# A third shifted copy of VectorE's attention tiles, made by GpSimd

## The chip, the cores and the metric

The kernel runs on one core of a Trainium2 chip. The metric is the device time of one execution in microseconds (us), as the median of several executions. The profile is that of one execution, and its times run from the first instruction.

Five engines work side by side, each with its own queue in a fixed order: TensorE (PE; PEld is its weight load), VectorE (DVE), ScalarE (ACT), GpSimd (POOL) and SyncE (SP), which here only starts transfers. They wait for one another on semaphores.

## The reference

Two pre-normalised layers on a sequence of 2048 tokens with 448 features. The first is attention with 16 query heads of 28 features that share one key and one value head. The second chooses 8 tokens by a score and sends them alone through a gated feed-forward net.

```
q = layernorm(x) @ wq            # 16 heads of 28
k, v = layernorm(x) @ wk, @ wv   # one head for all
p = softmax(q @ k.T / sqrt(28))
h = x + (p @ v) @ wo
r = layernorm(h) @ w_r           # 8 best of 2048 tokens
out = h + layernorm(h) + scatter(moe(layernorm(h)[best 8]))
```

Nearly all the time is spent in the scores, their exponential and the product with v: 16 x 2048 x 2048 exponentials.

## The kernel before, in words

**Blocks and tiles.** The attention is cut into 16 blocks (4 heads by 512 queries) and each block into 16 tiles of 128 keys. A tile is 4 heads x 512 queries on 128 partitions. TensorE computes its scores in two halves of 128 x 1024 (two matmuls each, helper line 371), somebody turns them into probabilities, and TensorE multiplies these with v (`Vs`) and adds them up in the bank of the block. A column of `Vs` holds the softmax's denominator.

**Two ways to the exponential.** Most tiles go to ScalarE: `act_unit` (line 880), one ACTIVATE for each half (line 884), written as `P`. Then one group of four products follows (`act_pv`). The others go to VectorE, which has no exponential: `dve_unit` (line 892) evicts each half as a clamped 16-bit integer (line 896) whose bits, read as bf16, are a rough power of two. Its error is smoothed with shifted copies: `shift` (line 900) adds a constant to the integers, and four variants v = 0 to 3, each multiplied with its own multiple of the values, are summed up by TensorE: `dve_pv` (line 907), four groups of four products for each such tile. The copies live in `Y`, with three buffers.

Before, VectorE makes the variants in two instructions (line 902): one of 2048 elements a partition (v = 1 from v = 0) and one of 4096 (v = 2 and 3 from v = 0 and 1).

**Which tiles.** `groups` (line 852) gives the number of VectorE tiles of a block: 4 in each block from 2 on, at the places of `where`; in blocks 0 and 1 together there are 5. That is 61 of 256 tiles; ScalarE has 195.

**Other work in a block.** VectorE also evicts the queries of a later block (`Q`, line 488) and the finished sums (`Ot`, line 658). `post_block` sends the denominators through memory (`Lc`, `Li`, `Rb`), and GpSimd keeps two checks (lines 668 and 670) and forms `On` = `Ot` x `Rb` (line 674). `out_proj` (line 687) makes four rows of the result from four `On` and does a layer norm: VectorE at lines 696 to 713, GpSimd for the power -0.5 (line 702). In the last block `last_pre` (line 793) and what follows it do this, followed by the feed-forward part.

**The order.** No engine's order is written out by hand. Each operation is told to a planner (`_Graph.op`) with an engine, an expected duration in ns, what it reads and writes, and a due time `prio`; 16 units of due time are one block. `plan` (line 79) is a list scheduler: an engine that is free takes, of the operations that are ready, the one with the earliest due time. The resulting order of each engine is fixed, and `finish` puts in the semaphores. At run time only the order counts, not the planned times. A second, exact version of the attention is in the program and is jumped over unless a check fails.

Of the kernel before, what the change touches and what calls it, by code (L numbers as in the profile page):

```python
# [7 lines left out]
ALU = mybir.AluOpType  # L8
# [10 lines left out]
class _Op:  # L19
    __slots__ = ("eng", "fns", "dur", "lat", "deps", "prio", "idx", "dma", "start", "end", "sig", "name", "nsucc",  # L20
                 "pred_left", "succs", "ready", "form")


class _Graph:
# [16 lines left out]
    def op(self, eng, fns, dur, reads=(), writes=(), prio=None, dma=False, acc=False, name="", form=0):  # L41
# [8 lines left out]
        o.form = form  # L50

# [27 lines left out]
    def plan(self):  # L79
# [16 lines left out]
        form = 0  # L96
        while left:
            best = None
            for e, lst in avail.items():
                if not lst:  # L100
                    continue
                t = free[e]
                now = [o for o in lst if o.ready <= t]
# [17 lines left out]
            free[e] = c.end  # L121
            orders[e].append(c)
# [120 lines left out]
def _main(nc, G, sb, ps, psb, flag, scr, xs, ptab, A_x, A_wq, A_wk, A_wv, A_wo, B_w_r, B_w_gate, B_w_up, B_w_down, out,  # L243
# [443 lines left out]
    def out_proj(qb, k):  # L687
# [3 lines left out]
        for g2 in range(0, 4, 2):  # L691
# [15 lines left out]
             reads=[("mv", t), ("h4", hr)], writes=[("h6", hr)])  # L707
        G.op(DV, lambda e: e.tensor_scalar(outf[:, t, :], h, st[:, t, 5:6], s6, ALU.mult, ALU.add), 420,  # L708
             reads=[("h", hr), ("st5", t), ("h6", hr)], writes=[("outf", t)])
        G.op(DV, lambda e: e.scalar_tensor_tensor(junk[:, :], h, s4, w_rb[:, :], ALU.mult, ALU.mult,  # L710
                                                  accum_out=st[:, t, 2:3]), 700,
             reads=[("h", hr), ("h4", hr), "w_rb"], writes=["junk", ("st2", t)])
        G.op(DV, lambda e: e.scalar_tensor_tensor(x_sb[:, t, D + 2:D + 3], s6, sw[:, 0:1], st[:, t, 2:3],
                                                  ALU.mult, ALU.add), 85,
             reads=[("h6", hr), "sw", ("st2", t)], writes=[("r", t)])
# [34 lines left out]
    def second_top():  # L750
        bank = misc_bank(15)
        if exact:
# [7 lines left out]
             reads=["iota96", "qsel", "prow"], writes=["ohq", "posc"])  # L760
# [8 lines left out]
        for src, dst, nm, rd in ((out[0, 0:1536, :], extc[:, 0:D], "extc", [("out", q, k) for q in range(3) for k in (1, 3)]),  # L769
# [5 lines left out]
                                           ALU.add), 420, reads=["hc"] + old, writes=["xnc"])  # L775

    def last_w():
        for g in range(4):
            G.op(DV, lambda e, g=g: e.scalar_tensor_tensor(junk[:, :], wo_pad[:, g, 0:D], 1.0, w_rb[:, :],
                                                           ALU.mult, ALU.mult, accum_out=wor[:, g:g + 1]), 600,  # L780
                 reads=["wo_pad", "w_rb", ("scr0", 3)] + wok, writes=["junk", ("wor", g)])
# [4 lines left out]
        for k in range(4):  # L786
            G.op(DV, lambda e, k=k: e.scalar_tensor_tensor(junk[:, :], x_sb[:, 12 + k, 0:D], 1.0, w_rb[:, :],
                                                           ALU.mult, ALU.mult, accum_out=xw[:, k:k + 1]), 600,
                 reads=[("x", 12 + k), "w_rb", ("scr0", 3)], writes=["junk", ("xw", k)])
# [62 lines left out]
    groups = [4] * NB  # L852
# [47 lines left out]
    def shift(m, v):  # L900
        n = m % NY
        G.op(DV, lambda e: e.tensor_scalar(Y[:, n, v:2 * v, :, :].bitcast(I16), Y[:, n, 0:v, :, :].bitcast(I16),  # L902
                                           v * STEP, None, ALU.add), 70 + 535 * v,
             reads=[("Y", n, 0, 0), ("Y", n, 0, 1)] + ([("Y", n, 1)] if v == 2 else []),
             writes=[("Y", n, 1)] if v == 1 else [("Y", n, 2), ("Y", n, 3)])
# [12 lines left out]
    for m, (b, j, t) in enumerate(dve_tiles):  # L918
        for p in range(2):
            at(t + 1.5 * p, dve_unit, m, b, j, p, t + 1.5 * p)  # L920
        for v in (1, 2):
            at(t + 1.6 + 0.5 * v, shift, m, v)
        for v in range(4):
            pv_list.append((t + 2.2 + 0.5 * v, dve_pv, m, v, b, j))
# [23 lines left out]
    at(16 * 2 + 2.5, q_project, 3, misc_bank(2))  # L948
# [255 lines left out]
```

## Time and profile before

| | |
|---|---|
| median of 3 runs | 404.59 us (404.42 to 405.1) |
| profiled execution | 403.72 us |
| its span, first to last instruction | 401.9 us |
| busy: ScalarE, VectorE, TensorE, GpSimd | 375.6, 354.8, 348.9, 62.2 us |
| granted TensorE clock, mean | 0.977 |

The profile's page gives the busy time of each engine, the costliest groups of instructions (line, engine, operation, output<-input, shapes, count, then busy time in us, mean ns of one, and the engine's idle time before them with what ended it), and the chain of work that ended last. Further views of the same trace are used: the timeline of one engine (start, duration, instruction, and in square brackets the idle time before it and what ended it; equal neighbours are merged, with their count), waits by releaser (total us, times, longest), and a table of stretches (for each, its length, then busy time and number of instructions of PE, PEld, DVE, ACT and POOL, the granted clock, the share of the DMA engines and GB/s). An instruction's duration overlaps with the next one's start, so its cost in a full queue is read from start to start.

### The profile page before, as it was taken

The page shows a single profiled execution, that of the slowest core. Times are in us where ns is not written, and L with a number is a line of the kernel's source. Part 1 is how long each engine was busy: PE and PEld are TensorE (multiplying, and loading weights), DVE is VectorE, ACT ScalarE, POOL GpSimd, SP SyncE. Part 2 cuts the span into 40 slices and gives each one's busy share as a digit, 9 for nine tenths or more (in the row PEclk, how much of TensorE's full clock was granted, in tenths as well). Part 3 has the DMA queues.
Part 4 walks back from the last instruction along what each step waited for, and adds up shares of the span by engine and source line. Part 5 has one row for each costly group of instructions (what it writes and reads, how often), then busy time and mean ns, then how long its engine had stood idle before and what let it go on. Part 6 is the DMA issues. An engine that isn't in the chain of part 4 may idle for free.

```text
span 401.9 us, 8036 instructions
## 1 busy us (share of the span) xinstructions
PE 348.9 (87%) x3367; PEld 109.9 (27%) x3367; DVE 354.8 (88%) x577; ACT 375.6 (93%) x423; POOL 62.2 (15%) x111
## 2 busy tenths in 40 slices
PE   7899889898897989989898989899898989789854
PEld 7333222222222222222222222222222222222244
DVE  6995799998899999898999899998989999999361
ACT  4999999999999999999999999999999999999761
POOL 8240001211001021101011111111020121206000
PEclk9999999999999999999999999999999999999955
DMA  7694000100010010110001000200001110111010
GB/s 195 175 246 148 1 2 3 56 3 27 2 31 0 6 48 3 42 36 27 25 29 47 22 31 5 72 2 29 27 27 47 44 44 19 49 46 32 1 43 14
DMA packets 18078, 17.14 MB, mean 43 GB/s; under 512 B 6684, under 2 KB 15156, under 8 KB 18036
## 3 DMA queue, kind: packets, MB, share of 16 engines
q1 hardware_dynamic: 17940, 16.55, 14.1%
q8 instruction: 27, 0.44, 0.5%
q14 instruction: 15, 0.12, 0.1%
q0 software_dynamic: 96, 0.03, 0.1%
HBM read 11.71 MB, written 4.86 MB: 41 GB/s over the span
## 4 chain that ended last, share of the span: by engine, by line
ACT 62%; PE 17%; DVE 17%; POOL 1%; issue 1%; DMA 1%; SPq 1%; POOLq 0%; DVEq 0%
ACT P L884 61%; PE ps L371 17%; DVE Y L896 7%; DVE Y L902 5%; DMA wv_sb<-in_A_wv_dram 1%; POOL hbuf L702 1%; SPq L385 1%; DVE Ot L658 1%; DVE bn L810 1%; DVE junk L710 0%; DVE hbuf L696 0%; DVE x_sb L708 0%; DVE Q L488 0%; DVE wo_pad L784 0%; DVE bn L698 0%
## 5 line engine op out<-in xcount | busy, mean ns | idle before, releaser
L884 ACT ACTIVATE P<-ps 128x1024 bf16<-128x1024 f32 x390 | 361.9, 1083 | 5.1 <-PE ps L371 3.9
L371 PE MATMUL ps<-Q,K 64*128 64x512 bf16 x1024 | 180.7, 384 | 35.9 <-ACT P L884 27.8
L896 DVE TENSOR_SCALAR Y<-ps 128x1024 int16<-128x1024 f32 x122 | 148.1, 1214 | 15.3 <-PE ps L371 15.1
L902 DVE TENSOR_SCALAR Y<-Y 128x2048 int16<-128x2048 int16 x122 | 119.1, 976 | 2.1
L371 PEld LDWEIGHTS ps<-Q,K 64*128 64x128 bf16 x1024 | 44.5, 93 | 179.1 <-ACT P L884 143.3
L371 PE MATMUL ps<-Y,Vs 128*32 128x512 bf16 x976 | 84.8, 383 | 2.9 <-DVE Y L902 2.9
L371 PE MATMUL ps<-P,Vs 128*32 128x512 bf16 x780 | 77.2, 388 | 0.0
L670 POOL TENSOR_TENSOR Ls<-Ls,Lc 128x16 f32<-128x16 f32 x15 | 9.9, 661 | 188.7 <-DMA Lc<-h_scr 188.7
L371 PEld LDWEIGHTS ps<-Y,Vs 128*32 128x32 bf16 x976 | 24.6, 95 | 32.4 <-issue 16.8
L371 PEld LDWEIGHTS ps<-P,Vs 128*32 128x32 bf16 x780 | 19.8, 93 | 43.2 <-issue 42.1
L674 POOL TENSOR_TENSOR On<-Ot,Rb 128x512 bf16<-128x512 f32 x15 | 19.2, 1283 | 76.7 <-DMA Rb<-h_scr 76.7
L371 PE MATMUL ps<-xnT,wq_pad 112*128 112x512 bf16 (+1 forms) x68 | 19.4, 371 | 0.4 <-DVE Ot L658 0.2
L371 PE MATMUL ps<-wo_pad,On 128*128 128x448 bf16 (+1 forms) x64 | 17.2, 358 | 1.5 <-DVE On L652 1.5
L702 POOL TENSOR_TENSOR hbuf<-st,nhalf 128x1 f32<-128x1 f32 x12 | 9.5, 791 | 20.2 <-DVE st L700 20.2
L488 DVE TENSOR_SCALAR Q<-ps,qone 128x512 bf16<-128x512 f32 x15 | 10.8, 717 | 1.1 <-PE ps L371 1.1
L658 DVE COPY Ot<-ps 128x512 f32<-128x512 f32 x15 | 10.2, 680 | 0.0
L710 DVE SCALAR_TENSOR_TENSOR junk<-hbuf,w_rb 128x448 bf16<-128x448 f32 x12 | 8.1, 677 | 0.0
L696 DVE TENSOR_TENSOR hbuf<-ps,x_sb 128x448 f32<-128x448 f32 x12 | 7.4, 618 | 0.8 <-PE ps L371 0.8
L371 PE MATMUL ps<-ident 128*128 128x128 bf16 x72 | 6.2, 253 | 1.8 <-POOL ident L400 1.8
L698 DVE BATCH_NORM_STATS2 bn<-hbuf 128x6 f32<-128x448 f32 x12 | 7.4, 617 | 0.1
L589 DVE BATCH_NORM_STATS2 bn<-x_sb 128x6 f32<-128x448 bf16 x12 | 7.0, 604 | 0.0
L371 PEld LDWEIGHTS ps<-wo_pad,On 128*128 128x128 bf16 x64 | 4.2, 97 | 9.5 <-issue 5.8
(185 smaller groups left out, 162.0 us busy)
## 6 DMA issues: line engine op xcount, KB each, us to landing
Rb<-h_scr SPq DMA_DIRECT2D x15, 256.0 KB
h_scr<-hbuf SPq DMA_DIRECT2D x12, 225.0 KB, 2.4
out_dram<-x_sb SPq DMA_DIRECT2D x8, 224.0 KB, 2.2
wg_sb<-in_B_w_gate_dram SPq DMA_DIRECT2D x1, 1568.0 KB, 11.4
wu_sb<-in_B_w_up_dram SPq DMA_DIRECT2D x1, 1568.0 KB, 17.7
wd_sb<-in_B_w_down_dram SPq DMA_DIRECT2D x1, 1568.0 KB, 21.0
x_sb<-in_A_x_dram SPq DMA_DIRECT2D x3, 448.0 KB, 5.6
x_sb<-in_A_x_dram SPq DMA_DIRECT2D x4, 112.0 KB, 2.3
```

The source lines that it names most:

```text
L371: return lambda e: e.matmul(o, lhsT=l, rhs=r, start=start, stop=stop)
L488: G.op(DV, lambda e: e.tensor_scalar(Q[:, b % 4, :], ps[:, bank, :], qone[:, 0:1], None, ALU.add), dvt(512), reads=[pk(bank), "qone"], wri ...
L658: G.op(DV, lambda e: e.tensor_copy(Ot[:, rb, :], ps[:, acc_bank(b), :]), dvt(512), reads=[pk(acc_bank(b))], writes=[("Ot", rb)], prio=u - 30)
L670: G.op(LE, lambda e: e.tensor_tensor(Ls[:, :], Ls[:, :], Lc[:, rb, :], ALU.add), 150, reads=["Ls", ("Lc", rb)], writes=["Ls"])
L674: G.op(PO, lambda e: e.tensor_tensor(On[:, qb % 2, g, :], Ot[:, rb, :], Rb[:, rb, :], ALU.mult), 1270, reads=[("Ot", rb), ("Rb", rb)], wri ...
L696: G.op(DV, lambda e: e.tensor_tensor(h, ps[:, bank, 0:D], x_sb[:, t, 0:D], ALU.add), dvt(D), reads=[pk(bank), ("x", t)], writes=[("h", hr)])
L698: G.op(DV, lambda e: e.bn_stats(bn6[:, t, :], h), dvt(D), reads=[("h", hr)], writes=[("bn6", t)])
L702: G.op(PO, lambda e: e.tensor_tensor(s4, st[:, t, 7:8], nhalf[:, 0:1], ALU.pow), 570, reads=[("st7", t), "nhalf"], writes=[("h4", hr)])
L710: G.op(DV, lambda e: e.scalar_tensor_tensor(junk[:, :], h, s4, w_rb[:, :], ALU.mult, ALU.mult, accum_out=st[:, t, 2:3]), 700, reads=[("h", ...
L884: G.op(AC, lambda e: e.activation(P[:, sl, :, :], ps[:, b0:b0 + 2, :], ACT.Exp, bias=EBIAS, scale=OCT), 905, reads=[pk(b0), pk(b0 + 1)], w ...
L896: G.op(DV, lambda e: e.tensor_scalar(Y[:, n, 0, p:p + 3:2, :].bitcast(I16), ps[:, 4:6, :], 0.0, 32639.0 - 3 * STEP, ALU.max, ALU.min), 114 ...
L902: G.op(DV, lambda e: e.tensor_scalar(Y[:, n, v:2 * v, :, :].bitcast(I16), Y[:, n, 0:v, :, :].bitcast(I16), v * STEP, None, ALU.add), 70 + ...
```

## The change

`shift` now makes each variant in an instruction of its own, always from v = 0 and as multiply by 1, then add. In blocks 2 and 4 to 15 the third (v = 3) runs on GpSimd, after VectorE's two. In block 3 and in the early tiles of blocks 0 and 1 all three stay on VectorE. Blocks 3, 5 and 9 get a fifth VectorE tile, in the place of a ScalarE tile. The products of a tile in the GpSimd blocks have later due times, the fourth most of all. The planner gets a flag `lock`: GpSimd's operations and the VectorE operations so marked are planned so that none starts before the one before it has ended. Marked are the shifts and several VectorE instructions of the layer norms and of the choice of tokens. The projection of block 3's queries is due 2.5 units later.

```diff
@@ _Graph.op
+        o.lock = (lock or eng == PO) and not dma
@@ _Graph.plan
+        port = 0.0
...
                 t = free[e]
+                for o in lst:
+                    if o.lock and o.ready < port:
+                        o.ready = port
...
             free[e] = c.end
+            if c.lock:
+                port = c.end
@@ out_proj, second_top, last_w: lock=True for VectorE's s6, outf, junk, r, ohq, xnc, wor, xw
-             reads=[("h", hr), ("st5", t), ("h6", hr)], writes=[("outf", t)])
+             reads=[("h", hr), ("st5", t), ("h6", hr)], writes=[("outf", t)], lock=True)
...
-    groups = [4] * NB
+    groups = [5 if b in (3, 5, 9) else 4 for b in range(NB)]
+    POB = [b for b in range(2, NB) if b != 3]
...
-    def shift(m, v):
+    def shift(m, v, b):
         n = m % NY
-        G.op(DV, lambda e: e.tensor_scalar(Y[:, n, v:2 * v, :, :].bitcast(I16), Y[:, n, 0:v, :, :].bitcast(I16),
-                                           v * STEP, None, ALU.add), 70 + 535 * v,
-             reads=[("Y", n, 0, 0), ("Y", n, 0, 1)] + ([("Y", n, 1)] if v == 2 else []),
-             writes=[("Y", n, 1)] if v == 1 else [("Y", n, 2), ("Y", n, 3)])
+        po = v == 3 and b in POB
+        G.op(PO if po else DV, lambda e: e.tensor_scalar(Y[:, n, v, :, :].bitcast(I16), Y[:, n, 0, :, :].bitcast(I16),
+                                                         1.0, v * STEP, ALU.mult, ALU.add), 2030 if po else 605,
+             reads=[("Y", n, 0, 0), ("Y", n, 0, 1)] + ([("Y", n, 1), ("Y", n, 2)] if po else []),
+             writes=[("Y", n, v)], lock=True)
...
-        for v in (1, 2):
-            at(t + 1.6 + 0.5 * v, shift, m, v)
+        for v in (1, 2, 3):
+            at(t + 1.6 + 0.5 * v, shift, m, v, b)
         for v in range(4):
-            pv_list.append((t + 2.2 + 0.5 * v, dve_pv, m, v, b, j))
+            pv_list.append((t + (4.2 if b in POB else 2.2) + 0.5 * v + (1.5 if v == 3 and b in POB else 0), dve_pv, m, v, b, j))
...
-    at(16 * 2 + 2.5, q_project, 3, misc_bank(2))
+    at(16 * 2 + 5.0, q_project, 3, misc_bank(2))
```

19 lines of the change are left out of this document (10 added, 9 removed).

## The prediction, made before the changed kernel ran

> **What bounds the kernel now.** I read the page first, for the engines' shares; then the timeline of ScalarE, to see whether it ever stops; then a table of stretches, one per block of attention; then the timelines of VectorE and GpSimd for single durations.
>
> ```profile
> PE 348.9 (87%) x3367; PEld 109.9 (27%) x3367; DVE 354.8 (88%) x577; ACT 375.6 (93%) x423; POOL 62.2 (15%) x111
> ...
> L884 ACT ACTIVATE P<-ps 128x1024 bf16<-128x1024 f32 x390 | 361.9, 1083 | 5.1 <-PE ps L371 3.9
> ...
> L896 DVE TENSOR_SCALAR Y<-ps 128x1024 int16<-128x1024 f32 x122 | 148.1, 1214 | 15.3 <-PE ps L371 15.1
> ```
>
> ScalarE works 93% of the span, nearly all of it in 390 exponentials (two for each of 195 tiles). It idled 5.1 us before them in all. VectorE has 122 evictions, so 61 tiles, and is at 88%: a close second. GpSimd is nearly free.
>
> ```profile
> 81.10 41.96 ACT L884 ACTIVATE P<-ps 128x1024 bf16<-128x1024 f32 x45 [0.55 <-PE ps L371]
> 123.48 202.08 ACT L884 ACTIVATE P<-ps 128x1024 bf16<-128x1024 f32 x218 [0.42 <-PE ps L371]
> ...
> 363.04 14.84 ACT L884 ACTIVATE P<-ps 128x1024 bf16<-128x1024 f32 x16 [0.84 <-PE ps L371]
> ```
>
> These rows merge back-to-back instructions. 218 exponentials ran in 202.08 us without a stop, so one costs 202.08/218 = 0.926 us on the path (the 1083 ns of the group overlap). A block of 12 ScalarE tiles costs 24 x 0.926 = 22.2 us, a block of 11 costs 20.4.
>
> The next rows are stretches between the Ot copies that close one block and the next: blocks 2, 3, 4, 5, 6, 9, 10 and 14. Columns: length, then busy time of PE, PEld, DVE, ACT, POOL.
>
> ```profile
> 66.20:87.00 20.80, 19.32 (x180) 5.14 (x178) 20.17 (x24) 19.39 (x22) 4.53 (x6) 1.00 0.09 30
> 87.00:108.90 21.90, 18.93 (x182) 4.92 (x178) 19.41 (x22) 21.83 (x25) 2.24 (x3) 1.00 0.05 14
> 108.90:132.10 23.20, 19.89 (x182) 5.46 (x182) 22.34 (x38) 22.66 (x26) 1.97 (x3) 1.00 0.04 13
> 132.10:154.70 22.60, 20.20 (x186) 5.38 (x184) 21.67 (x31) 22.48 (x25) 3.22 (x4) 1.00 0.08 24
> 154.70:176.70 22.00, 19.98 (x184) 5.32 (x184) 20.84 (x30) 21.92 (x25) 3.02 (x4) 1.00 0.10 35
> ...
> 221.10:243.20 22.10, 19.95 (x186) 5.49 (x184) 20.59 (x31) 22.09 (x25) 3.08 (x4) 1.00 0.08 25
> 243.20:265.40 22.20, 20.05 (x186) 5.45 (x184) 20.80 (x30) 22.13 (x25) 2.91 (x4) 1.00 0.10 34
> ...
> 333.20:358.40 25.20, 21.94 (x201) 6.14 (x201) 24.76 (x47) 24.54 (x28) 3.73 (x5) 1.00 0.12 40
> ```
>
> In blocks 5 to 10 ScalarE is full and VectorE has 1 to 1.5 us to spare. ScalarE misses time only where VectorE is fuller still: 1.41 us in block 2 (20.80 - 19.39), 0.54 in block 4, 0.66 in block 14. So time is bought with ScalarE tiles, and VectorE must have room for them.
>
> **The change, part by part.**
>
> *A. Three tiles leave ScalarE.* Three blocks get a fifth VectorE tile: 6 exponentials x 0.926 = **-5.56 us**, as long as nothing else becomes late.
>
> *B. What a tile costs VectorE.* One tile in a contiguous stretch:
>
> ```profile
> 60.30 1.22 DVE L896 TENSOR_SCALAR Y<-ps 128x1024 int16<-128x1024 f32 x1
> 61.55 0.69 DVE L902 TENSOR_SCALAR Y<-Y 128x2048 int16<-128x2048 int16 x1
> 62.16 1.22 DVE L896 TENSOR_SCALAR Y<-ps 128x1024 int16<-128x1024 f32 x1
> 63.29 1.22 DVE L902 TENSOR_SCALAR Y<-Y 128x4096 int16<-128x4096 int16 x1
> 64.42 0.68 DVE L658 COPY Ot<-ps 128x512 f32<-128x512 f32 x1
> ```
>
> From start to start: 1.25 us for an eviction whose result the next instruction needs, 0.61 for a pass of 2048, 1.13 for an eviction followed by other work, 1.13 for a pass of 4096. Now a tile is 1.13 + 1.25 + 0.61 + 1.13 = 4.12. After, with the third copy on GpSimd: 1.13 + 1.25 + 2 x 0.61 = 3.60 (-0.52). All on VectorE (blocks 0, 1, 3): 3 x 0.61 makes 4.21 (+0.09). That the passes now multiply by 1 and then add I cost at nothing; the bounds are nothing and a doubled pass, 0.6 each. I take nothing, since the form and tile are those of the 0.61 row.
>
> Over the kernel: 52 old tiles x -0.52, 9 x +0.09, new tiles 4.21 + 2 x 3.60 give about -15 us of VectorE work. The distribution matters more. Block 3: 19.41 + 4 x 0.09 + 4.21 = 24.0 in 21.9 - 1.85 = 20.05, **3.9 over**. Block 5: 21.67 - 4 x 0.52 + 3.60 = 23.2 in 20.75, 2.4 over. Block 9: 22.1 in 20.25, 1.9 over. Each can borrow from its neighbours, since scores and exponentials of the next block don't need this block's sum: block 2 has 20.80 - 18.1 = 2.7 free, block 4 23.2 - 20.3 = 2.9, blocks 6 and 10 3.2 and 3.5. Blocks 2 to 4 together want 62.3 of 64.05, 97%, where they now take 94%. Now VectorE at 96 to 97% (blocks 2 and 4) went with 0.5 to 1.4 us lost on ScalarE. I give back **+0.8** for block 3 and **+0.4** for 5 and 9 together; the bounds are nothing and the whole overrun, 8.2.
>
> *C. The copy on GpSimd.* Nothing of this shape runs there now. The nearest rows:
>
> ```profile
> L605 POOL TENSOR_SCALAR xn<-x_sb,nmean,rstd 128x448 bf16<-128x448 bf16 x5 | 3.7, 742 | 0.4 <-POOL rstd L595 0.2
> L428 POOL COPY wq_pad<-wq_sb 112x448 bf16<-112x448 bf16 x3 | 1.6, 556 | 0.3 <-DMA wq_sb<-in_A_wq_dram 0.3
> L418 POOL MEMSET wq_pad<- 128x2048 bf16 x1 | 1.8, 1794 | 0.0
> L674 POOL TENSOR_TENSOR On<-Ot,Rb 128x512 bf16<-128x512 f32 x15 | 19.2, 1283 | 76.7 <-DMA Rb<-h_scr 76.7
> ...
> 6.79 0.28 POOL L430 COPY wv_pad<-wv_sb 112x112 bf16<-112x112 bf16 x1 [0.76 <-DMA wv_sb<-in_A_wv_dram]
> ```
>
> Two copies, of 112 and 448 elements, differ by 0.28 us in 336 elements, 0.82 ns each. The two-step tensor_scalar of 448 took 0.742; 1600 elements more give 2.05 us. The floor is the memset of 2048, 1.79; the ceiling is the two-input row, 1.283 x 4 = 5.1. I take **2.05**, by the row of the same operation.
>
> The Trainium skill, "GPSIMD Engine Reference", section "Engine selection", sends elementwise work to VectorE, though it calls one-input work roughly line-rate; section "Performance versus the Vector engine" has loops from 1.03 to 1.8 cycles per element at 1.2 GHz, which would make an estimate of 1.8 to 3.1 us for this copy. By the upper figure the occupation worked out in D would be 21.9 of 22.2 us in a four-tile block and 26.4 of 20.4 in a five-tile one: 12 us over in the two such blocks that use GpSimd, or about 411. That is an estimate by the page, and the shape of the third rival.
>
> *D. Exclusion.* Where the two engines now meet, one waits:
>
> ```profile
> 77.38 2.90 DVE L902 TENSOR_SCALAR Y<-Y 128x2048 int16<-128x2048 int16 x2
> ...
> 144.88 1.50 DVE L902 TENSOR_SCALAR Y<-Y 128x4096 int16<-128x4096 int16 x1
> ...
> 77.81 1.39 POOL L674 TENSOR_TENSOR On<-Ot,Rb 128x512 bf16<-128x512 f32 x1 [5.69 <-DMA Rb<-h_scr]
> 145.26 1.54 POOL L702 TENSOR_TENSOR hbuf<-st,nhalf 128x1 f32<-128x1 f32 x1
> 159.88 0.22 POOL L668 TENSOR_TENSOR Lsi<-Lsi,Li 128x16 f32<-128x16 f32 x1 [0.17 <-DVE Li L662]
> ...
> 181.71 0.22 POOL L670 TENSOR_TENSOR Ls<-Ls,Lc 128x16 f32<-128x16 f32 x1 [13.28 <-DMA Lc<-h_scr]
> ...
> 192.44 0.55 POOL L702 TENSOR_TENSOR hbuf<-st,nhalf 128x1 f32<-128x1 f32 x1 [2.45 <-DVE st L700]
> ```
>
> A pair of passes took 2.90 instead of 0.61 + 1.22 while L674 ran from 77.81 to 79.20; a GpSimd op of 0.55 took 1.54 while a pass ran. So I treat the two as one resource. In a four-tile block: 4 x (1.22 + 0.2 + 2.05) = 13.9, where 0.2 is the hand-over (0.17 us from VectorE to L668 above); GpSimd's own L670, L668, L674, L702 0.22 + 0.22 + 1.28 + 0.55 = 2.3; VectorE's layer-norm passes
>
> ```profile
> L710 DVE SCALAR_TENSOR_TENSOR junk<-hbuf,w_rb 128x448 bf16<-128x448 f32 x12 | 8.1, 677 | 0.0
> ...
> L708 DVE TENSOR_SCALAR x_sb<-hbuf,st 128x448 bf16<-128x448 f32 x12 | 6.1, 508 | 0.0
> ```
>
> take 1.19, and with two small ones, which I put at 0.3, 1.5. That makes 17.7 of 22.2 us. In a five-tile block 21.2 of 20.4: tight again, and covered by the neighbours. The copy starts when VectorE's two passes are done, and what VectorE does next, two evictions (1.13 + 1.25), covers a copy of 2.05 + 0.2. That cover is what the planner arranges; I cost D at nothing, and where it fails, at up to 2.05 a tile, which the 3.5 us that VectorE then has free in a block (22.2 - 20.8 + 4 x 0.52) pay for once or twice a block.
>
> *E. Waits.* TensorE takes its instructions in a fixed order, and the fourth product of a tile now waits for GpSimd; behind it stand the scores that feed ScalarE.
>
> ```profile
> PEld ps L371 <- DVE Y L902: 11.4, 25, 1.0
> ...
> POOL On L674 <- DMA Rb<-h_scr: 76.7, 15, 6.5
> ...
> 361.72 0.62 PE L371 MATMUL ps<-Y,Vs 128*32 128x512 bf16 x8
> ```
>
> Such waits exist already (25, 11.4 us) and ScalarE hardly feels them. On GpSimd's queue the copies stand behind L674, which today sits up to 6.5 us for a transfer; the plan has to put it behind the copies. TensorE gets 9 more groups of products (+12, -3), at 0.31 a group at most (8 matmuls in 0.62) 2.8 us, in blocks where it is at 20 of 22.1. Bounds for E: nothing to 0.5 for each of 14 blocks, 7 us; I put it at nothing beyond the give-back of B, by those 25 waits.
>
> *F. Late blocks and tail.* VectorE's relief (2.1 us a block) should return part of what ScalarE loses in blocks 13 to 15 (0.66 in block 14, 0.84 in 15): **-0.8**, bounds nothing and -2.0. On the other side the last product of block 14 comes some 2 us later (2.05 + 0.2 + 0.61 instead of 1.13), so Ot, its transfers and On too:
>
> ```profile
> 369.84 1.27 POOL L674 TENSOR_TENSOR On<-Ot,Rb 128x512 bf16<-128x512 f32 x1 [0.50 <-DMA Rb<-h_scr]
> ...
> 372.10 0.56 PE L371 MATMUL ps<-wo_pad,On 128*128 128x450 bf16 x2
> ...
> 377.95 0.61 PE L371 MATMUL ps<-P,Vs 128*32 128x512 bf16 x8
> ```
>
> On ends 6.8 us ahead of the last products, and 16 output matmuls follow: **+0.5**, bounds nothing and 2.0.
>
> Sum: -5.56 + 0.8 + 0.4 - 0.8 + 0.5 = -4.66. The profiled execution took 403.72 (span 401.9 plus 1.8): 399.06. The median is 0.87 above that execution: **399.9 us**.
>
> **Rivals.**
>
> *1. VectorE becomes the bound in the five-tile blocks.* If only half of the 8.2 us of overrun is borrowed, 4.1 replaces my 1.2: -1.8, **402.8**. For: the 97% of blocks 2 to 4. Against: idle room on both sides, exponentials that can run ahead.
>
> *2. It doesn't do what it says.* The copy leaves VectorE, but TensorE's in-order wait for it gives the time to ScalarE as gaps: 0.35 us in each of 14 blocks is 4.9, **404.8**, no change. For: ScalarE's few stops are all released by TensorE. Against: 25 waits that cost little now.
>
> *3. The shared resource decides, and it is slower.* With a copy of P us a four-tile block needs 4 x (P + 1.42) + 3.8; that is 22.2 at P = 3.2. Beyond it blocks follow the copies. The tensor_scalar row scaled in proportion (0.742 x 2048/448) gives P = 3.4: ten blocks of 23.1 and two of 27.9 are 286.8 instead of 12 x 22.2, +20.4, less 1.85 in block 3: **423**. For: 0.742 could be mostly per element. Against: copy and memset rows at 0.8 to 0.9 ns an element.
>
> The Trainium skill, "SBUF — State Buffer", section "Who interferes with whom", says that issue order decides who is blocked, for a whole instruction. The trace agrees (2.90 us), and no run here shows yet how often the planned order holds.
>
> **How the numbers follow.** Forecast, 398.4 to 401.6: 0.56. Better still (nothing given back): 0.06. Rival 1, to 403.8: 0.14. Rival 2: 0.07. Rival 3: 0.17. A change under 0.2%, 0.8 us, can't be told from none: faster 0.76, same 0.07, slower 0.17. The range leaves out rival 3 and half of the better case: 397.8 to 404.6.
>
> **What would show it.** Right: 384 exponentials at 0.926 without new stops; L902's successor at 0.61 apart, 138 on VectorE and 54 on GpSimd at about 2.05; VectorE near 340 us busy. Wrong: passes of 1.5 to 2.9 us on VectorE while GpSimd copies; ScalarE idle well over 5 us before its exponentials, in blocks 3 to 5 above all (rival 1) or spread evenly behind TensorE waits for GpSimd (rival 2); GpSimd copies over 3 us (rival 3).

## The result and the profile after

The kernel before took 403.75 us (median of 22 executions, 402.21 to 405.1), the changed kernel 402.40 (22, 400.45 to 403.73). The ratio is **0.9968**, 95% interval 0.9956 to 0.998: a gain of 0.32%, 1.3 us. The forecast was 4.7 us. The sign was right, and the size came out at less than a third. Ratios here and below leave out executions in a slower state of the chip (two of six of e8, one of twelve of e14), so the ratio of e8 is less than its median says.

The profiled execution of the changed kernel took 401.65 us, its span is 399.8. First the groups that answer to those quoted of before (line numbers are eight or ten higher: L893 is the exponential, L905 the eviction, L912 the shift, L718 the layer-norm pass):

```profile
PE 352.0 (88%) x3403; PEld 111.0 (28%) x3403; DVE 342.4 (86%) x599; ACT 369.6 (92%) x417; POOL 165.7 (41%) x165
...
L893 ACT ACTIVATE P<-ps 128x1024 bf16<-128x1024 f32 x384 | 355.9, 1084 | 7.2 <-PE ps L379 6.5
L905 DVE TENSOR_SCALAR Y<-ps 128x1024 int16<-128x1024 f32 x128 | 155.9, 1218 | 25.6 <-PE ps L379 25.1
L912 POOL TENSOR_SCALAR Y<-Y 128x2048 int16<-128x2048 int16 x54 | 104.2, 1929 | 104.5 <-DVE Y L912 96.4 <-DVE st L708 7.9
L912 DVE TENSOR_SCALAR Y<-Y 128x2048 int16<-128x2048 int16 x138 | 93.7, 704 | 0.4
L718 DVE SCALAR_TENSOR_TENSOR junk<-hbuf,w_rb 128x448 bf16<-128x448 f32 x12 | 9.9, 822 | 0.0
```

The work is where the forecast put it: 384 exponentials, 54 copies of 1.93 us on GpSimd (2.05 forecast), VectorE at 342.4 us (near 340 forecast). Yet ScalarE idled 7.2 us ahead of its exponentials instead of 5.1, and L718 has a mean of 822 ns instead of 677.

Where ScalarE stopped, from its timeline (start, duration, instruction, count, and the idle time before it):

```profile
68.45 2.85 ACT L893 ACTIVATE P<-ps 128x1024 bf16<-128x1024 f32 x3 [1.41 <-PE ps L379]
71.46 32.39 ACT L893 ACTIVATE P<-ps 128x1024 bf16<-128x1024 f32 x35 [0.16 <-PE ps L379]
104.49 16.61 ACT L893 ACTIVATE P<-ps 128x1024 bf16<-128x1024 f32 x18 [0.64 <-PE ps L379]
...
348.94 1.02 ACT L893 ACTIVATE P<-ps 128x1024 bf16<-128x1024 f32 x1 [0.21 <-PE ps L379]
350.55 1.02 ACT L893 ACTIVATE P<-ps 128x1024 bf16<-128x1024 f32 x1 [0.59 <-PE ps L379]
352.07 1.02 ACT L893 ACTIVATE P<-ps 128x1024 bf16<-128x1024 f32 x1 [0.49 <-PE ps L379]
353.33 18.44 ACT L893 ACTIVATE P<-ps 128x1024 bf16<-128x1024 f32 x20 [0.24 <-PE ps L379]
372.58 1.02 ACT L893 ACTIVATE P<-ps 128x1024 bf16<-128x1024 f32 x1 [0.81 <-PE ps L379]
377.52 0.72 ACT L654 ACTIVATE Rb<-Ot 128x256 f32<-128x256 f32 x2 [3.91 <-DVE Ot L650]
```

The same instruction in the kernel before, whose last exponential ended at 363.04 + 14.84 = 377.88:

```profile
379.62 0.72 ACT L646 ACTIVATE Rb<-Ot 128x256 f32<-128x256 f32 x2 [1.75 <-DVE Ot L642]
```

From Rb both kernels have the same 22.28 us to the end (401.9 - 379.62, 399.8 - 377.52). So two numbers hold the whole difference. The last exponential ends at 373.60 instead of 377.88, 4.28 earlier. **The gap from it to Rb**, the tail in what follows, grew from 1.74 to 3.92. There is no crowd of stops in blocks 3 to 5. The stops are in block 14 (348 to 354) and at the very end, with two single ones before: 0.64 at 104.49 in block 3, and 1.41 at 68.45, where block 2 begins. The last is in every version with the new order of work, also in e7 below, which has no copy on GpSimd.

Block 14, on GpSimd and VectorE:

```profile
344.11 1.27 POOL L682 TENSOR_TENSOR On<-Ot,Rb 128x512 bf16<-128x512 f32 x1
345.36 1.89 POOL L912 TENSOR_SCALAR Y<-Y 128x2048 int16<-128x2048 int16 x1
```

```profile
345.33 2.40 DVE L718 SCALAR_TENSOR_TENSOR junk<-hbuf,w_rb 128x448 bf16<-128x448 f32 x1
```

The copy began right behind On, and the layer-norm pass that VectorE had up at that moment took 2.40 us instead of 0.68. TensorE, whose rows come next, then paused three times within 3.1 us, the first time behind ScalarE and twice behind VectorE. A table of stretches shows its granted clock (the column after the five busy times) at half from 350 to 352:

```profile
346.96 0.39 PE L379 MATMUL ps<-Q,K 64*128 64x512 bf16 x2 [0.53 <-ACT P L893]
...
348.34 0.24 PE L379 MATMUL ps<-ident,x_sb 128*12 128x128 bf16 x1 [0.67 <-DVE x_sb L721]
...
349.48 1.04 PE L379 MATMUL ps<-Q,K 64*128 64x512 bf16 x4 [0.58 <-DVE Y L905]
```

```profile
350.00:352.00 2.00, 2.00 (x18) 0.29 (x14) 1.88 (x4) 1.02 (x1) 0.00 (x0) 0.50 0.01 0
```

And the end of the span, GpSimd's queue and then TensorE's:

```profile
365.01 3.42 POOL L779 DMA_INDIRECT xnT<-out_dram,idc  x1 [0.22 <-issue]
368.74 0.86 POOL L779 DMA_INDIRECT xnT<-h_scr,idc  x1 [0.30 <-issue]
369.64 1.91 POOL L912 TENSOR_SCALAR Y<-Y 128x2048 int16<-128x2048 int16 x1
371.51 1.28 POOL L682 TENSOR_TENSOR On<-Ot,Rb 128x512 bf16<-128x512 f32 x1
```

```profile
371.60 0.61 PE L379 MATMUL ps<-Y,Vs 128*32 128x512 bf16 x8 [1.22 <-POOL Y L912]
...
373.45 0.75 PE L379 MATMUL ps<-wo_pad,On 128*128 128x450 bf16 x3
...
375.84 0.40 PE L379 MATMUL ps<-P,Vs 128*32 128x512 bf16 x4
```

A copy stands behind 4.6 us of indirect transfers, TensorE waits 1.22 us for it (and ScalarE 0.81 behind that), and On comes at 371.51 instead of 369.84. Before, the first of the four groups of output matmuls that need On began at 372.10, beside the last exponentials. Now three of the four, 373.45 to 375.84, stand between the last exponential and the last products.

So the theory to test: the copy and the fifth tiles do what was forecast, and the loss has three places, **the hold** in block 14, **the indirect transfers** in GpSimd's queue, and **the output matmuls** behind a late On. Rivals: VectorE is full in the five-tile blocks after all, or the exclusion costs everywhere.

### The profile page after: what moved, and what is told of

Read it like the earlier page. It is cut to its first block, busy times and chain, and to the rows that moved or that the text cites. A ratio compares the mean times of both kernels' runs of the same rounds, so it can differ in the third digit from the quotient of the medians.

```text
span 399.8 us, 8174 instructions
## 1 busy us (share of the span) xinstructions
PE 352.0 (88%) x3403; PEld 111.0 (28%) x3403; DVE 342.4 (86%) x599; ACT 369.6 (92%) x417; POOL 165.7 (41%) x165
## 4 chain that ended last, share of the span: by engine, by line
ACT 53%; PE 23%; DVE 14%; DMA 4%; POOL 2%; issue 2%; SPq 2%; POOLq 0%; DVEq 0%
ACT P L893 53%; PE ps L379 23%; DVE Y L905 6%; DVE Y L912 3%; DMA x_sb<-in_A_x_dram 2%; SPq L393 2%; DMA w_rb<-in_B_w_r_dram 1%; POOL xnT L779 1%; DMA Lc<-h_scr 1%; DVE Ot L666 1%; DVE junk L718 1%; DVE bn L818 1%; POOL Y L912 1%; DMA h_scr<-Ot 0%; DVE On L660 0%
## 5 line engine op out<-in xcount | busy, mean ns | idle before, releaser
L893 ACT ACTIVATE P<-ps 128x1024 bf16<-128x1024 f32 x384 | 355.9, 1084 | 7.2 <-PE ps L379 6.5
L905 DVE TENSOR_SCALAR Y<-ps 128x1024 int16<-128x1024 f32 x128 | 155.9, 1218 | 25.6 <-PE ps L379 25.1
L912 POOL TENSOR_SCALAR Y<-Y 128x2048 int16<-128x2048 int16 x54 | 104.2, 1929 | 104.5 <-DVE Y L912 96.4
L912 DVE TENSOR_SCALAR Y<-Y 128x2048 int16<-128x2048 int16 x138 | 93.7, 704 | 0.4
L379 PE MATMUL ps<-Y,Vs 128*32 128x512 bf16 x1024 | 92.3, 386 | 1.8 <-POOL Y L912 1.2
L678 POOL TENSOR_TENSOR Ls<-Ls,Lc 128x16 f32<-128x16 f32 x15 | 4.1, 272 | 52.6 <-DMA Lc<-h_scr 52.6
L710 POOL TENSOR_TENSOR hbuf<-st,nhalf 128x1 f32<-128x1 f32 x12 | 11.9, 990 | 14.9 <-DVE st L708 14.9
L676 POOL TENSOR_TENSOR Lsi<-Lsi,Li 128x16 f32<-128x16 f32 x15 | 6.2, 416 | 9.0 <-DVE Li L670 8.9
L718 DVE SCALAR_TENSOR_TENSOR junk<-hbuf,w_rb 128x448 bf16<-128x448 f32 x12 | 9.9, 822 | 0.0
L603 POOL TENSOR_TENSOR rstd<-var,nhalf 128x4 f32<-128x4 f32 x3 | 3.1, 1029 | 11.6 <-DVE nmean L605 11.6
```

Source lines behind the costliest of these rows:

```text
L379: return lambda e: e.matmul(o, lhsT=l, rhs=r, start=start, stop=stop)
L676: G.op(LE, lambda e: e.tensor_tensor(Lsi[:, :], Lsi[:, :], Li[:, rb, :], ALU.add), 150, reads=["Lsi", ("Li", rb)], writes=["Lsi"])
L710: G.op(PO, lambda e: e.tensor_tensor(s4, st[:, t, 7:8], nhalf[:, 0:1], ALU.pow), 570, reads=[("st7", t), "nhalf"], writes=[("h4", hr)])
L893: G.op(AC, lambda e: e.activation(P[:, sl, :, :], ps[:, b0:b0 + 2, :], ACT.Exp, bias=EBIAS, scale=OCT), 905, reads=[pk(b0), pk(b0 + 1)], w ...
L905: G.op(DV, lambda e: e.tensor_scalar(Y[:, n, 0, p:p + 3:2, :].bitcast(I16), ps[:, 4:6, :], 0.0, 32639.0 - 3 * STEP, ALU.max, ALU.min), 114 ...
L912: G.op(PO if po else DV, lambda e: e.tensor_scalar(Y[:, n, v, :, :].bitcast(I16), Y[:, n, 0, :, :].bitcast(I16), 1.0, v * STEP, ALU.mult, ...
```

## The experiments

Each ratio is to the kernel before on the same chip; the change stands at 0.9968 [0.9956, 0.998]. These edits move work, its due time or a wait; none leaves any work out. Versions are compared by these ratios, since they ran on different chips.

### The parts of the change

**e4, the copy without the fifth tiles.**

```diff
-    groups = [5 if b in (3, 5, 9) else 4 for b in range(NB)]
+    groups = [4] * NB
```

> Four VectorE tiles in every block as before, the third copy on GpSimd as in the change. Theory A: the loss at the end is there and the 5.56 us of ScalarE work are not saved: 3.5 to 4.3 us slower than before, ratio 1.008 to 1.011. Theory B (the loss belongs to the fifth tiles): about as before, 0.997 to 1.001. Theory C: 1.008 to 1.011 too, but with ScalarE's stops spread evenly over the blocks.

Measured 402.12 us, 0.9951 [0.9939, 0.9964]: as fast as the change, with 390 exponentials, and faster than any of the three theories had it. ScalarE's timeline:

```profile
11.73 55.62 ACT L893 ACTIVATE P<-ps 128x1024 bf16<-128x1024 f32 x60 [0.52 <-PE ps L379]
...
294.78 80.37 ACT L893 ACTIVATE P<-ps 128x1024 bf16<-128x1024 f32 x87 [0.17 <-PE ps L379]
377.92 0.72 ACT L654 ACTIVATE Rb<-Ot 128x256 f32<-128x256 f32 x2 [2.77 <-DVE Ot L650]
```

The last 87 exponentials run without a stop. From the first to the last they take 363.4 us, against 366.5 before (11.35 to 377.88): VectorE's relief is worth 3.1 us by itself, and the tail takes 1.0 back. In the change as it is, then, the three tiles bring nothing.

Most of the 3.1 us is in the late blocks. Before, the row

```profile
325.96 21.03 ACT L884 ACTIVATE P<-ps 128x1024 bf16<-128x1024 f32 x22 [0.40 <-PE ps L371]
```

has 0.956 us for each exponential, against 80.37/87 = 0.924 in e4. From first exponential to first exponential, blocks 13 to 15 take 2.6 us less in e4 and blocks 0 to 4 take 1.4 less; blocks 5 to 12 take 0.95 more.

**e7, the fifth tiles without the copy.**

```diff
-    POB = [b for b in range(2, NB) if b != 3]
+    POB = []
```

> The fifth tiles of blocks 3, 5 and 9 with all passes on VectorE, no copy on GpSimd at all. Theory (a fifth tile needs room on VectorE, and the copy is what makes it): VectorE is over by 3.9, 5.5 and 4.9 us in the three blocks (21.67 + 4 x 0.09 + 4.21 = 26.2 in 20.75 for block 5, 25.2 in 20.25 for block 9), its neighbours have 1 to 2.7 us each, so most of the 5.56 us comes back as stops of ScalarE in blocks 3 to 6, 9 and 10: 403.5 to 407. Rival (ScalarE is the only bound and VectorE's share does not matter): 404.2 - 5.56 + 1 = 399.6.

Measured 408.8 us, 1.0119 [1.0097, 1.0141], above the range: without room on VectorE a tile costs more than it saves. Two rows of its ScalarE:

```profile
148.42 3.77 ACT L893 ACTIVATE P<-ps 128x1024 bf16<-128x1024 f32 x4 [1.68 <-PE ps L379]
153.84 13.35 ACT L893 ACTIVATE P<-ps 128x1024 bf16<-128x1024 f32 x14 [1.65 <-PE ps L379]
```

These stops are in and behind block 5; the change has none over 0.65 us between 72 and 345.

**e8, the same copies, planned without exclusion.**

```diff
-        o.lock = (lock or eng == PO) and not dma
+        o.lock = False
```

> The change with the planner told of no exclusion: the same copies on GpSimd and the same fifth tiles, planned as if the two engines never met. Theory (the exclusion is only a plan, but it does hold for most copies): without it VectorE's passes and GpSimd's copies meet often, passes of 1.5 to 2.9 us appear by the dozen (each hold up to 2 us, some 30 to 60 of them) and some blocks lose 1 us or more on ScalarE: 404 to 412. Rival (engines' real times drift from the plan so much that it orders nothing, or VectorE's spare time of 3.5 us a block pays for all holds): 401.4 to 403.4, like the change.

Measured 417.44 us (the median of all six), 1.028 [1.0223, 1.0336], with ScalarE idle 19.1 us, above the range:

```profile
L893 ACT ACTIVATE P<-ps 128x1024 bf16<-128x1024 f32 x384 | 358.7, 1059 | 19.1 <-PE ps L379 17.8
...
L912 DVE TENSOR_SCALAR Y<-Y 128x2048 int16<-128x2048 int16 x138 | 104.9, 779 | 1.2
```

The order planned with the exclusion is worth 13 us by the ratios (1.028 - 0.9968 of 404). VectorE's passes average 779 ns instead of 704, 17 of them over 0.9 us instead of 3. But the length of the passes alone is not the loss, for in e4, with four tiles a block, they are longer still:

```profile
L912 DVE TENSOR_SCALAR Y<-Y 128x2048 int16<-128x2048 int16 x131 | 103.1, 806 | 1.2
```

There 19 of 131 took over 0.9 us, up to 2.38, and ScalarE idled 3.7 us in all: VectorE had the room to pay for them. How much of e8's 13 us the holds cost, and how much the other order of work, is open.

### The hold in block 14

**e15, the change with GpSimd bound to the plan.** Each GpSimd operation of the exclusive kind waits for the VectorE pass that the plan has ahead of it; the order on every engine is unchanged.

```diff
             if c.lock:
                 port = c.end
+                if pl is not None and pl.eng != c.eng and c.eng == PO and not self.after:
+                    c.deps[pl.idx] = True
+                pl = c
```

> The change with one thing added: each GpSimd operation waits on a semaphore for the VectorE pass that the plan has ahead of it. Theory (the copy of block 14 that starts ahead of the layer-norm pass, the 2.40 us hold and the stops of ScalarE behind it, 0.59 + 0.49 + 0.24 there, are a cost of their own): the hold goes (0.7 us), the stops between 350 and 354 us go, 0.6 to 1.5 us faster than the change (ratio to before 0.993 to 0.995); the stop near 372 us and the tail stay. Rival (the hold is harmless, what counts is the place of the transfers and of the matmuls): within 0.4 us of the change.

Measured 399.81 us, **0.99** [0.9876, 0.9924]: 2.7 us better than the change, more than expected. GpSimd, VectorE and ScalarE of this kernel (its lines are four higher):

```profile
346.02 1.90 POOL L916 TENSOR_SCALAR Y<-Y 128x2048 int16<-128x2048 int16 x1 [1.26 <-DVE x_sb L725]
```

```profile
344.69 0.67 DVE L722 SCALAR_TENSOR_TENSOR junk<-hbuf,w_rb 128x448 bf16<-128x448 f32 x1
```

```profile
336.79 32.19 ACT L897 ACTIVATE P<-ps 128x1024 bf16<-128x1024 f32 x35 [0.18 <-PE ps L383]
369.98 1.02 ACT L897 ACTIVATE P<-ps 128x1024 bf16<-128x1024 f32 x1 [1.00 <-PE ps L383]
374.91 0.72 ACT L658 ACTIVATE Rb<-Ot 128x256 f32<-128x256 f32 x2 [3.91 <-DVE Ot L654]
```

The copy now comes after the layer-norm pass, which is back at 0.67 us, and 35 exponentials run without a stop through block 14; from the same exponential in block 13 (its row starts at 315.22 in the change, at 314.38 here) to the end of the last one it is 1.8 us shorter. The stop of 1.00 and the tail of 3.91 stay, as expected.

Those 1.8 us are not the hold alone, since TensorE's clock fell behind it. e13 (below) has the change's order in block 14, the same hold and the same three pauses of TensorE, and there the clock stayed at 1.00:

```profile
345.85 2.40 DVE L718 SCALAR_TENSOR_TENSOR junk<-hbuf,w_rb 128x448 bf16<-128x448 f32 x1
```

```profile
350.00:352.00 2.00, 2.00 (x22) 0.55 (x22) 1.97 (x6) 1.84 (x3) 0.00 (x0) 1.00 0.17 56
```

From that exponential of block 13 to the end of the last but one, the change took 56.55 us, e13 55.42 and e15 54.60. So the hold costs 0.8 us, and the fall of the clock that followed it in the change 1.1 more. Other runs repeat all three: e2, with hold and fall, took 56.51, e9, with the hold alone, 55.42, and the bound e10 and e11 54.60. Another 0.7 us of e15's gain lies in block 3, where in the change a pass of a five-tile block was held by On, not by a copy, ahead of the stop of 0.64:

```profile
99.63 2.37 DVE L912 TENSOR_SCALAR Y<-Y 128x2048 int16<-128x2048 int16 x2
100.05 1.40 POOL L682 TENSOR_TENSOR On<-Ot,Rb 128x512 bf16<-128x512 f32 x1 [6.21 <-DMA Rb<-h_scr]
```

The same hold and stop are in e6, e12 and e13; e2, e9 and e16 have neither, though nothing binds them, so this part is not sure to be e15's own.

**e6, no GpSimd copies in block 14** (with the transfers moved, as in e2 below).

```diff
-    POB = [b for b in range(2, NB) if b != 3]
+    POB = [b for b in range(2, NB) if b not in (3, 14)]
```

> The selection due 9 units later, and block 14 without GpSimd copies (its third passes on VectorE). Theory (in block 14 a copy that starts just ahead of a layer-norm pass of VectorE holds it 1.8 us, TensorE pauses, and its clock falls to about half for 3 us): the pass of 2.40 us is back at about 0.7 us, the clock between 346 and 353 us stays above 0.9, ScalarE has no stops there, and the time falls by 1 to 1.5 us against 400.09: 398.5 to 399.2. Rival (block 14 lacks room on VectorE, 2.1 us fewer now, and that makes ScalarE stop as in the kernel before): 400.0 to 401.5, with stops of ScalarE of 0.6 us or more in block 14 behind VectorE's passes.

Measured 401.42 us, 0.9925 [0.9906, 0.9943], 1.4 us slower than e2. My theory missed and its rival was right:

```profile
347.81 6.52 ACT L893 ACTIVATE P<-ps 128x1024 bf16<-128x1024 f32 x7 [0.56 <-PE ps L379]
355.59 18.44 ACT L893 ACTIVATE P<-ps 128x1024 bf16<-128x1024 f32 x20 [1.26 <-PE ps L379]
```

The hold of 2.40 us is gone (a pass of 1.70, held by On, stands at 345.29), and without the copies' relief VectorE stops ScalarE for longer, 0.56 and 1.26. The copies of block 14 are worth having; what is bad is one that starts out of turn.

### The transfers and the matmuls

**e2, the selection of tokens, and the indirect transfers with it, due 9 units later.**

```diff
-    at(16 * 15 + 5.0, second_top)
+    at(16 * 15 + 14.0, second_top)
```

> Block 15's copies stay on GpSimd, but the choice of the 8 tokens is due 9 units later, so that GpSimd's two indirect transfers come behind its last copy instead of ahead of the last two. Theory A in its narrow form (the indirect transfers, 3.42 and 0.86 us long there, hold up the copies): TensorE's wait of 1.2 us for a copy near the end goes, ratio 0.991 to 0.994. If the copies themselves and the output product behind them are late in any case: 0.996 to 0.997. Theories B and C: 0.996 to 0.998.

Measured 400.09 us, 0.9891 [0.9877, 0.9906], 3.1 us better than the change, more than expected. The transfers now stand behind the last copy, the first takes 1.15 us instead of 3.42, and the stop of 0.81 is gone. That is 1.1 us in the profiled execution, from the last but one exponential to the last (0.90 instead of 2.01); where the rest of the 3.1 comes from is open. The tail is still 3.81.

**e5, the same with four tiles everywhere.** Both edits, those of e2 and e4.

> All four tiles a block (no fifth tile), the copies on GpSimd as in the change, and the query selection (the two indirect transfers with it) due 9 units later, as in the version with only the selection moved (400.09). Theory (the three fifth tiles are good, and what ate them was the place of the indirect transfers and the late blocks): with four tiles the selection was in nobody's way, since the version with the copy alone has no long hold in block 15, so moving it brings little: 401.3 to 402.2, and the tiles are then worth 1.2 to 2.1 us. Rival (the fifth tiles are paid back by VectorE in their own blocks, and moving the selection relieves every version alike): 402.1 less 2.3, so 399.6 to 400.2, and the tiles are worth nothing.

Measured 402.13 us, 0.9949 [0.9931, 0.9966], as e4: with four tiles the transfers were in nobody's way. Between e5 and e2 lie the three tiles alone, 2.3 us by the ratios.

**e14, the kernel before with the due times of e2 and e9.**

> The kernel before with the same two due times altered (selection 9 units later, 16 output matmuls at 18). Theory (these two were harmless before and harmful only with the copies in GpSimd's queue): within 0.8 us of the kernel before, or slower by up to 1.5, since the matmuls that ran beside the last exponentials now run behind them. Rival (the moves help any version): 2 to 4 us faster than before.

Measured 404.17 us, 1.0006 [0.9986, 1.0025], tail 1.62. These due times are worth nothing without the change, so what they give back in e2 and e9 is the change's own loss.

**e9, the output matmuls later too.**

```diff
-    at(16 * b + (14.6 if k else 17.0) + 0.1 * k, last_pre, k)
+    at(16 * b + 18.0 + 0.1 * k, last_pre, k)
```

> The selection due 9 units later, and the 16 matmuls that put three quarters of the last output rows together (those of the other three head groups) due at 18 in block 15 instead of 14.6, so that most of them stand behind the last products. Theory (these matmuls, put off by the late On of block 14, stand ahead of the last products after the last exponential and make up the longer tail): the gap from the last exponential to Rb, 3.81 us in the version with only the selection moved and 3.92 in the change, shrinks to 2.4 to 2.9, and the time to 398.9 to 399.3. Rival (what the matmuls free is paid behind On, where they now stand ahead of the last output product): the gap shrinks but the distance from Rb to the end grows by as much, and the time stays at 399.8 to 400.3.

Measured 399.31 us, 0.9882 [0.9853, 0.9912]: its interval covers that of e2. The profile has the tail at 2.88, and the way from Rb to the end no longer than in e2 (22.62, 22.73):

```profile
349.24 21.44 ACT L893 ACTIVATE P<-ps 128x1024 bf16<-128x1024 f32 x23 [0.16 <-PE ps L379]
373.56 0.72 ACT L654 ACTIVATE Rb<-Ot 128x256 f32<-128x256 f32 x2 [2.88 <-DVE Ot L650]
```

**e13, the matmuls alone** (e9's edit without e2's).

> The change with one due time altered: the 16 output matmuls at 18 in block 15 instead of 14.6; the selection stays where it was. Theory (the longer tail, 3.92 us from the last exponential to Rb against 1.74 in the kernel before, is these matmuls standing ahead of the last products): the gap falls to 2.6 to 3.0 and the time by 0.8 to 1.2 us against the change, to about 401.4 beside 402.4 (ratio to before 0.993 to 0.995). Rival (the tail is set by the last GpSimd copy, which the indirect transfers put off): gap stays at 3.5 or more, time within 0.4 us of the change.

Measured 401.04 us, 0.9924 [0.9906, 0.9942], somewhat more gain than expected. The profile does not show it in the expected way: its tail is 4.91, with TensorE at a granted clock of 0.56 there.

```profile
373.00:376.00 3.00, 3.00 (x21) 0.63 (x14) 1.54 (x1) 0.26 (x1) 1.30 (x1) 0.56 0.02 5
```

That execution took 402.37, the slowest of six, so the run speaks for the matmuls by its time only.

**e16, no copies in block 15, the transfers moved as in e2.**

```diff
-    POB = [b for b in range(2, NB) if b != 3]
+    POB = [b for b in range(2, NB - 1) if b != 3]
```

> The selection 9 units later, and block 15 without GpSimd copies (third passes on VectorE), the 16 matmuls where the change has them. Theory (the copies of block 15 put On of block 14 off, and with it the 16 matmuls and the last products): On starts 2 us or more ahead of 368.59, the gap from the last exponential to Rb falls from 3.81 to 1.7 to 2.4, 1.0 to 1.8 us faster than the version with the selection moved alone: ratio to before 0.985 to 0.987. Rival (block 15 needs VectorE's room more than an early On): gap falls, but ScalarE stops by as much in block 15, ratio 0.988 or more.

Measured 400.92 us, 0.993 [0.9915, 0.9944]. GpSimd, then ScalarE:

```profile
367.27 1.83 POOL L682 TENSOR_TENSOR On<-Ot,Rb 128x512 bf16<-128x512 f32 x1 [6.30 <-DMA Rb<-h_scr]
```

```profile
358.29 14.77 ACT L893 ACTIVATE P<-ps 128x1024 bf16<-128x1024 f32 x16 [2.12 <-PE ps L379]
374.80 0.72 ACT L654 ACTIVATE Rb<-Ot 128x256 f32<-128x256 f32 x2 [1.74 <-DVE Ot L650]
```

On waits only for its transfer, 1.3 us earlier than in e2 (2 or more expected), and the tail is 1.74, that of the kernel before to a hundredth. So the longer tail comes from block 15's copies. That it comes by way of On and the matmuls behind it is argued; e9 shows 0.9 us of it that way. But the stop of 2.12 at the start of block 15, which e1 has too (2.11), takes more than the tail gives: the rival was right. Block 15 needs the room as well.

**e1, e3, an early and unclean form of the same question:** no copies in block 15 (e1), in 14 and 15 (e3), with the transfers where they were.

> The third copy of block 15's four tiles is back on VectorE; all else is the changed kernel, whose ratio to before is 0.9968. Theory A (the gain is lost at the end: GpSimd's queue in blocks 14 and 15): in the changed kernel 3.9 us lie between the last exponential and the last block's reciprocal, before 1.7; this returns some 2 us, ratio 0.990 to 0.993, and the gap is under 2.2 us. Theory B (VectorE is the bound around the five-tile blocks 3, 5 and 9): no gain, 0.996 to 0.999. Theory C (small TensorE waits for GpSimd's copies spread over all blocks): a gain of one block in 14, under 0.3 us, 0.996 to 0.997.

> Blocks 14 and 15 keep all copies on VectorE. Theory A: beside the 2 us of the end it returns what block 14 lost when a copy held a VectorE instruction for 1.8 us, TensorE paused and its granted clock fell to 0.50 for 3 us: ScalarE's stops in block 14 go from 1.7 to about 0.6 us, the mean clock from 0.97 to 0.98, ratio 0.986 to 0.991. Theory B: 0.997 or above, since VectorE gets more work. Theory C: 0.995 to 0.997.

Measured 404.43 us, 1.0008 [0.9997, 1.002], and 404.07, 0.9998 [0.9976, 1.0019]. Both missed, and they decide nothing about the copies: the planner made another order, in which VectorE waits for an indirect transfer ahead of the last tile (row of e1).

```profile
368.85 1.19 DVE L782 TENSOR_SCALAR xnT<-xnT 8x448 bf16<-8x448 f32 x1 [2.76 <-DMA xnT<-h_scr,idc]
```

### Versions that go further

**e11 and e10, e9 with GpSimd bound to the plan (e11), or both engines bound (e10).**

> Like e10, but only GpSimd waits (for the planned VectorE pass ahead of it); VectorE never waits for GpSimd. Theory: the hold of the layer-norm pass in block 14 goes (the copy can no longer start ahead of it), the clock there stays above 0.9: 0.5 to 1.2 us faster than e9. Rival (the hold is not what costs in block 14, or each copy comes later by its wait and TensorE's product behind it too): within 0.5 us of e9 or slower.

> Like the version with the selection and the 16 output matmuls moved (e9), with the planned exclusion made binding: wherever the plan has a GpSimd operation of the exclusive kind next after a VectorE one, or the reverse, the later waits on a semaphore for the earlier. Order of instructions on each engine unchanged. Theory (copies that start a little ahead of their planned turn and hold VectorE's pass are a cost of 1 to 1.5 us, in block 14 above all): passes of 1.5 us and more on VectorE vanish, block 14 has no stops, 0.5 to 1.5 us faster than e9. Rival (binding the order makes VectorE wait for GpSimd operations that stand behind a transfer, as On and the row sums do, and a wait costs more than a hold): slower than e9 by 1 to 8 us, with VectorE waiting for GpSimd before its passes in most blocks.

e11: 399.08 us, **0.9864** [0.9835, 0.9893], the lowest of all, 5.5 us below the kernel before, though not told apart from e9 by its interval. Its theory is not shown: in e9's profiled execution the hold stands at 344.44 (2.40 us), the clock behind it is at 1.00, and ScalarE loses no more than 0.21 us at a time there. e10: 400.02 us, 0.9886 [0.9857, 0.9916], no faster than e9, against its theory. Bound on both sides, no pass is longer than 0.9 us, and VectorE idles 5.3 us ahead of its passes, 4.9 of them for GpSimd, as the rival has it though for less time:

```profile
L916 DVE TENSOR_SCALAR Y<-Y 128x2048 int16<-128x2048 int16 x138 | 90.6, 681 | 5.3 <-POOL Y L916 2.6 <-POOL On L686 1.6 <-POOL Ls L682 0.7
```

**e12, e9 with a fifth tile in blocks 7 and 11 too.**

```diff
-    groups = [5 if b in (3, 5, 9) else 4 for b in range(NB)]
+    groups = [5 if b in (3, 5, 7, 9, 11) else 4 for b in range(NB)]
```

> Like e9, with a fifth tile in blocks 7 and 11 too, so 4 more exponentials off ScalarE, 4 x 0.926 = 3.70 us. If VectorE is not the bound in five-tile blocks (my theory: three of them gave 2.0 us net of 5.56 in the change's late blocks' company, the rest lost at the end of the span and not in those blocks): 1.5 to 2.7 us faster than e9. Rival (VectorE and the shared port are full where five-tile blocks alternate with four-tile ones: 23.2 and 18.7 of 20.3 and 22.2 us, 98.6% of each pair): no faster than e9, with new stops of ScalarE of 0.5 us or more in blocks 5 to 12.

Measured 406.47 us, 1.0046 [1.0029, 1.0064], 7 us slower than e9: my theory missed badly. From 190 to 331 us stops of 0.3 to 1.1 us follow one another, as its rival had it, such as this one:

```profile
230.79 18.45 ACT L893 ACTIVATE P<-ps 128x1024 bf16<-128x1024 f32 x20 [1.00 <-PE ps L379]
```

Whether VectorE's room is the reason is open. From 231 to 256 us VectorE was busy 21.3 us of 25, so not full, and ahead of the stop of 1.10 us at 250.34 TensorE was at work on the projection of Q. What is shown is the limit: the tiles of blocks 3, 5 and 9 pay, two more do not.

## Why the prediction was right in sign and wrong in size

*A, C, right.* 384 exponentials at 0.925 us (32.39 us for 35 in the row at 71.46), and a copy of 1.93 us. The third rival, priced at over 3.2 us a copy, is out.

*B, right.* With the order bound (e15) the exponentials take 359.7 us (11.33 to 371.00), with the copy alone (e4, not bound) 363.4: the tiles are worth 3.75 there, against 5.56 - 1.2 = 4.36 forecast. The first rival does not describe this change (stops of 0.64 us at most in blocks 3 to 5), though e7 shows that without the copy it would have.

*F, the relief, undersized.* Forecast -0.8 with a bound of -2.0, measured -3.1 (e4), of which -2.6 in blocks 13 to 15. I read their loss from the stops, 0.66 and 0.84, and not from the exponentials between the stops, which stood at 0.956 us there instead of 0.926. Blocks 0 to 4, which I had not credited, gave 1.4 more, and 5 to 12 took 0.95.

*D, the step that failed.* I wrote that the cover "is what the planner arranges" and cost the exclusion at nothing, since VectorE's free time would pay. Measured: +2.85 (the exponentials take 362.5 us in the change, 359.7 in e15). The order between the two engines exists in the plan only. In block 14 a copy started 0.03 us after the pass it was to follow had come up (345.36 and 345.33), and held it. Of the 2.85, 1.9 is in block 14 (0.8 for the hold, 1.1 for the clock that fell behind it, which it did not in e9, e13 and e16), 0.7 in block 3, which some unbound versions escape too, and 0.35 in the first 60 exponentials, ahead of any copy, which the change does not explain; the last stop, 1.00 instead of 0.81, takes some 0.1 to 0.2 off. VectorE's free time does pay where there is some: e4, with four tiles everywhere, has 19 long passes and no loss from them that shows. It does not in a five-tile block and in block 14, where TensorE pauses behind VectorE. e15 shows that binding the order takes the loss of block 14 away; e8 gives no price for a hold. The Trainium skill, "SBUF — State Buffer", section "Who interferes with whom", has it that issue order decides which of the two stands still, for the whole instruction. That one of them stood still for a whole copy, the 2.40 us row agrees with; the order of issue it leaves open, since the pass that was held has the earlier start, 345.33, while On was still at work until 345.38.

*E, put at nothing, right but for the end.* TensorE's weight loads waited for a copy only three times, which leaves no room for the second rival, waits spread evenly over the blocks:

```profile
PEld ps L379 <- POOL Y L912: 2.0, 3, 1.5
```

The wait near the end, behind the indirect transfers, is the stop of 0.81 us.

*F, the tail, undersized.* Forecast +0.5 with a bound of 2.0, measured +2.18 (3.92 - 1.74). I counted the delay of block 14's last product, but not that On would queue behind block 15's copies, nor that 4.6 us of indirect transfers are in the same queue. Of GpSimd's queue I had counted only L674's wait. e16 gives the whole 2.1 us of the tail back, e9 0.9 of it.

Together: -3.1 - 3.75 + 2.85 + 2.18 = -1.8, beside the -2.1 between the two spans (the exponentials start 0.27 earlier). The terms are steps from version to version (before, e4, e15, the change), so they add up by construction, and each holds what its profiled execution happened to have. Three terms that I put at less than 1 us were 2 to 3 us each: one gain and two losses. Two counts were off without weight: 13 blocks use GpSimd, not 14 (the second rival), and 11 of them have four tiles, not 10 (the third, which would give 424).

What e15 and e2 give back is not additive: 2.7 and 3.1 us alone, 4.2 with e9's edit in e11 (0.9968 - 0.9864 of 404).

## What to carry to other kernels

When two engines exclude each other, an order that is only planned fails where it is closest, and that costs time where neither has room, as in block 14; where there was room (e4) it cost nothing that shows. A wait on the side that can afford it (here GpSimd) took the flip away and cost little, while binding both sides gained nothing more. When work is moved onto an idle engine, list everything that already stands in its queue near the end of the kernel, transfers it issues among them, and what comes after each. And a part that frees time on the second-busiest engine can be worth more than the part that uses it: run the two apart.

## What the runs showed of the hardware

- In the change the clock fell to 0.50 after three pauses of 0.53, 0.67 and 0.58 us; in e13 it stayed at 1.00 after three of 0.53, 0.67 and 0.57. In e13 it fell after one of 1.47 us (0.56 over 373 to 376), while after 1.22 us at 371.60 in the change and 1.41 at 369.00 in e15 it did not. So the length of the pauses alone does not decide it. Mean clocks of the change were 0.971 to 0.973 in 19 of 22 executions (median 402.59 us) and 0.979 to 0.980 in three (400.45 to 401.12). Of e15's six, the two at 0.980 took 398.18 and 398.44, so its gain is there at equal clocks too. The Trainium skill, "TensorE: Matmul & The Clock Gate", section "What's actually happening", names an idle window of about 3.4 us, free-running; by that alone no pause here is long enough. Its section "A second HAM failure mode: psum-queue depth-cycling" has the clock fall with frequent short pauses; the change agrees with that, e13's block 14 does not.
- Issuing the first indirect transfer kept GpSimd 3.42 us while VectorE made four passes of 2048 (2.48 us), and 1.15 us in e2 and e16 with none beside it. The Trainium skill, "SBUF — State Buffer", section "Who interferes with whom", says that a transfer held up by VectorE is one whose descriptors GpSimd makes; these rows agree.
- A multiply and add of 2048 int16 takes GpSimd 1.90 us undisturbed (0.93 ns an element) and VectorE 0.61.
